# A two-layer attention and MLP kernel: the list scheduler gives way to written-out orders of each engine and a written-out list of PSUM banks

## The chip, the core and the metric

The kernel runs on one core of a Trainium2 chip. The core has five engines that run side by side, each through its own list of instructions in order: TensorE (PE in the profile, with PEld for its weight loads), VectorE (DVE), ScalarE (ACT), GpSimd (POOL) and SyncE (SP), which here issues every DMA. They wait for each other through semaphores. The metric is the device time of one execution in microseconds; lower is better. A measurement here is the median of several executions.

## What is computed

Input x is one sequence of 2048 rows of 576 bfloat16 numbers. Two layers are applied, each an attention block and an MLP block with residuals and the same weights in both layers:

```python
x = x + A(layernorm(x), wqkv, wo)
x = x + B(layernorm(x), w1, b1, w2, b2)     # and both once more

# A: 32 heads of 18, causal with a window of 256 keys
qkv = x @ wqkv
scores = q @ k^T * 18 ** -0.5, masked to 0 <= i - j < 256
o = softmax(scores) @ v, heads joined, @ wo
# B: layernorm again, then 576 -> 4608 -> 576
h = gelu(layernorm(x) @ w1 + b1)
out = h @ w2 + b2
```

## The kernel before, in words

**Tiles and chunks.** The 2048 rows are 16 tiles of 128; four tiles make a chunk, so there are eight chunks, 0 to 3 of the first layer and 4 to 7 of the second (`CH`). The residual x stays in SBUF in float32 (`x_res`), both layers run in one launch.

**What one chunk does.** The names are those of the stages in the code.

- `ln1`, `ln_stats`, `ln_rstd`, `ln_norm_T` (L690 to L749): layernorm. DVE takes mean and variance, POOL the reciprocal root, DVE writes the normalised tile `xn`, and a DMA turns it into `xnTa` (for attention) or `xnTm` (for the MLP). For the four tiles of the first chunk PE turns them instead (L742) and ACT copies them out of PSUM (L745).
- `qkv` (L838 to L885): q, k and v of a tile. In chunks 0 and 1 each is two halves of 288 columns with five matmuls (kinds f and c below, L804, L785, L788); from chunk 2 on each is two phases of row-halved matmuls (kind h, L844) where the second phase (`own=True`) waits for the first. DVE or ACT casts the halves into `qn` or `vA`, and a DMA turns q and k (L884); the k of the first chunk are turned on PE (L878) and copied by ACT (L882).
- `E`, `E0` with `scores` and `pv` (L900 to L1018): attention, for eight groups of heads in three parts. A `scores` task writes two pairs of PSUM banks (L913), ACT takes two exps of them (L922), POOL masks them (L943), and a `pv` task (L960) multiplies by v. DVE then transposes, divides and transposes again.
- `tail` (L1033): the product with wo, the residual add (L1023), and the second layernorm.
- `G_part` (L1055 to L1101), three times per chunk, `ga`, `gb`, `gc`: twelve blocks of w1 in kind h (L1080), each followed by a gelu on ACT (L1090). Two phases again, of 10 and 8 matmuls per task.
- `mm2` (L1103 to L1138), `ma`, `mb`, `mc`: the product with a third of w2, in two tasks of six blocks for each half of the columns, and the residual add on DVE.

The stages of neighbouring chunks are woven: while the attention of chunk k runs, the MLP of chunk k-1 and the projections of k+1 fill PE.

**Kinds of matmul task.** Every PE task has a `mode`: f (whole array), r (four row groups, `scores`), h (two row halves) or c (column groups: `pv`, `mm2`, `tail` and chunk 1's projections). A c task other than `pv` may also run as whole-array matmuls ("wide", L785) or as quads of four 32-column matmuls (L788), which the end of `schedule` chooses: runs of c tasks without a `pv`, and the parts of a run ahead of its first and behind its last `pv` when they sum to over 4 us, become wide.

**What sets the order.** `Plan.add` (L209) only collects tasks: what each reads and writes, an estimated cost and latency, a priority and the PSUM banks that it may have. `Plan.schedule` (L263 to L414) then simulates the engines: it takes again and again the task that can start first, with ties settled by `prio`, to which `PL.nudge` (L483 to L552) adds a number per stage, and `place` gives it the bank that is free earliest. Chains (`fifo`) hold the feeding matmuls and ACT's work in order of their listing; `starves` holds back tasks that would delay them before a planned 40 us; `turn` makes a change of kind dearer; `SWITCH` is its cost. Where PE would stand still in the plan for over 0.4 us before 140 us, `keep_warm` (L249) puts matmuls on zeros (`warm_fn`, L687). The tasks are then handed, sorted by their planned start, to the five lists, and `Sched.add` (L65) derives the semaphore waits from what they read and write. On the chip only the order within each list and the banks are left of the plan.

**The start.** SP issues the loads of x tile 0, x tile 1, the q weights (3 issues), the k weights (3), x tiles 2 and 3, the v weights (3), then x tiles 4 to 7. DVE clears `warm`, `ident`, and parts of wqkv and wo; PE then clears PSUM banks 7, 6, 5 and 4 with two matmuls each (`zero`, L675) and runs fillers.

Of the kernel before, what the change touches and what calls it, by code (L numbers as in the profile page):

```python
# [159 lines left out]
class Task:  # L160
    __slots__ = ("idx", "eng", "fn", "reads", "writes", "cost", "lat", "prio", "dma", "ring", "handles", "alloc", "move", "desc",
                 "npred", "succ", "ready", "end", "plain", "fifo", "hold", "stage", "mode", "own", "port", "wide")
# [24 lines left out]
class Plan:  # L187


    def __init__(self, S, nbanks):  # L190
        self.S = S
        self.tasks = []
        self.lw = {}
        self.rd = {}
        self.nbanks = nbanks
        self.warm_fn = None
        self.warm_from = 0.0
        self.warm_until = 0.0
        self.feed_until = 0.0
        self.turn = {}  # L200
        self.turn_from = 0.0
        self.ring = RING
        self.stage = ""
        self.part = ""
        self.chain = None
        self.nudge = {}
        self.fifo_last = {}

    def add(self, eng, fn, reads=(), writes=(), dma=None, ring=4, cost=0.1, lat=0.1, prio=0.0, alloc=(), fifo=None, plain=False, after=(), move=0.0, desc=0, hold=False, mode="f", own=False, port=None, wide=None):  # L209
        if eng == "dve" and fifo is None:  # L210
            fifo = self.chain
        stage = self.stage + self.part + ("+" if dma in ("w1", "w2", "xr") else "")
        prio += self.nudge.get(stage, 0.0)
        t = Task(idx=len(self.tasks), eng=eng, fn=fn, reads=tuple(reads), writes=tuple(writes), cost=cost, lat=lat, prio=prio,
                 dma=dma, ring=ring, alloc=tuple(alloc), handles=tuple({r for r in tuple(reads) + tuple(writes) if isinstance(r, Bank)}),
                 plain=plain, move=move, desc=desc, fifo=fifo, hold=hold, stage=stage, mode=mode, own=own,
# [16 lines left out]
        order = set()  # L233
        if fifo is not None:
            if fifo in self.fifo_last:
                order.add(self.fifo_last[fifo])
            self.fifo_last[fifo] = t
        order -= pred
        for p in pred:
            p.succ.append((t, True))  # L240
        for p in order:
            p.succ.append((t, False))
        t.npred = len(pred) + len(order)
# [5 lines left out]
    def keep_warm(self, a, b, bank_free, extra):  # L249

        if self.warm_fn is None or a < self.warm_from:
            a = max(a, self.warm_from)
        n = int((b - a - 0.1) * 0.8 / (0.165 if a < 7 else 0.115))
        banks = [x for x in (7, 6, 5, 4) if bank_free.get(x, 1e9) <= a]
        if n < 1 or not banks:
# [4 lines left out]
                 dma=None, ring=4, alloc=(), handles=(), plain=False, move=0.0, desc=0, fifo=None, hold=False, stage="", mode="f", own=False, port=False, wide=None)  # L260
        extra.append((a, t))

    def schedule(self):  # L263
        free = {e: BEGIN for e in ENGS}
        mode = "f"
        port = 0.0
        released = {e: [] for e in ENGS}
        for t in self.tasks:
            if t.npred == 0:
                released[t.eng].append(t)  # L270
        bank_free = {b: 0.0 for b in range(self.nbanks)}

        def place(t):

            got = []
            taken = set()
            when = 0.0
            for h in t.alloc:
                best = None
                for n, c in enumerate(h.choices):  # L280
                    bs = (c, c + 1) if h.pair else (c,)
                    if any(b in taken or b not in bank_free for b in bs):
                        continue
                    key = (max(bank_free[b] for b in bs), n)
                    if best is None or key < best[0]:
                        best = (key, c, bs)
                if best is None:
                    return None, None
                got.append(best[1])
                taken.update(best[2])  # L290
                when = max(when, best[0][0])
            return got, when

        feed = [t for t in self.tasks if t.fifo == "pa"]
        fed = 0
        backlog = 0.0

        def cost(t):
            return t.cost + (SWITCH if t.eng == "pe" and t.mode != mode else 0.0)

        def starves(t, st, got):

            if fed == len(feed) or feed[fed].npred:
                return False
            f = feed[fed]
            where, when = place(f)
            if where is None:
                return False
            at = max(free["pe"], f.ready, when)
            end = st + cost(t)  # L310
            late = end if at < end else at
            if t.alloc and set(got) & {b for w, h in zip(where, f.alloc) for b in ((w, w + 1) if h.pair else (w,))}:
                late = max(late, end + 0.65)
            return late > at and late + f.cost + f.lat > max(free["act"], st) + backlog

        order = []
        extra = []
        queued = {}
        served = {}
        turned = {}  # L320
        n = len(self.tasks)
        while len(order) < n:
            best = None
            cands = []
            for e in ENGS:
                for t in released[e]:
                    st = max(free[e], t.ready)
                    if t.port:
                        st = max(st, port)
                    got = ()  # L330
                    if t.alloc:
                        got, when = place(t)
                        if got is None:
                            continue
                        st = max(st, when)
                    key = (int((st + (self.turn.get(mode + t.mode, 0.0) if e == "pe" and st >= self.turn_from else 0.0)) * 1000 + 0.5), t.prio, t.idx)
                    if e == "pe":
                        cands.append((key, t, st, got))
                    if best is None or key < best[0]:
                        best = (key, t, st, got)  # L340
            assert best is not None, "stuck"
            _, t, st, got = best
            if t.eng == "pe" and t.fifo is None and st < self.feed_until and starves(t, st, got):
                for c in sorted(cands, key=lambda c: c[0]):
                    if c[2] < self.feed_until and (c[1].fifo is not None or not starves(*c[1:])):
                        _, t, st, got = c
                        break
            if t.eng == "pe":
                t.cost, mode = cost(t), t.mode
            if t.eng == "pe" and st < self.warm_until and st - free["pe"] > 0.4:  # L350
                self.keep_warm(free["pe"], st, bank_free, extra)
                free["pe"] = st
            released[t.eng].remove(t)
            for h, no in zip(t.alloc, got):
                h.no = no
                for b in h.banks():
                    del bank_free[b]
            free[t.eng] = st + t.cost
            if t.port:
                port = st + t.cost  # L360
            if t.fifo == "pa":
                fed += 1
                backlog += sum(x.cost for x, data in t.succ if data and x.eng == "act")
            elif t.fifo == "act" and t.handles:
                backlog -= t.cost
# [958 lines left out]
```

## Time and profile before

| | |
|---|---|
| median of 3 runs | 862.02 us (861.75 to 862.07) |
| span of the profiled execution, first to last instruction | 860.3 us |
| its own time beside the span | not given separately; the median of the runs stands 1.7 us above the span |
| PE busy | 849.0 us (99%), 11684 matmuls |
| ACT busy | 594.1 us (69%) |
| DVE, POOL busy | 393.9 us, 377.9 us |
| DMA moved | 119.78 MB, mean 139 GB/s |
| granted PE clock, mean over the span | 1.000 |

The profile describes one execution. A busy time is the union of the instructions of an engine; matmuls are pipelined, so a busy PE is not PE at its peak. "Idle before" is the time in which an engine had nothing running just ahead of an instruction, with the event that ended it. The chain of waits follows the work that ended last back to the start. The costliest groups are the MLP's first product and ACT's exps:

```profile
L1080 PE MATMUL ps<-xnTm,w_sb 64*128 64x512 bf16 x2592 | 289.2, 376 | 0.7 <-DVE x_res L1023 0.6
L922 ACT ACTIVATE pT<-ps 128x1024 bf16<-128x1024 f32 (+1 forms) x384 | 346.6, 973 | 59.3 <-PE ps L913 58.4
```

### The profile page before, as it was taken

To read this page: it belongs to the slowest core of one execution; us is meant where nothing else is said; L and a number is where in the kernel's file an instruction comes from. 1 tells how busy PE (TensorE), PEld (TensorE's weight loads), DVE (VectorE), ACT (ScalarE), POOL (GpSimd) and SP (SyncE) were. 2 spreads that over 40 slices of the span, in tenths; PEclk is the share of its full clock that TensorE was granted. 3 is DMA by queue.
4 is the path that set the end of the run, shared out by engine and by line. 5 is a ranking of instruction groups with operands and counts; after the bars stand their busy time and mean duration, and the time that the engine had idled before them with its cause. 6 is when DMAs were issued, how large, how long until landed. Compare 5 with 4: busy or idle time off the path is not lost.

```text
span 860.3 us, 27204 instructions
## 1 busy us (share of the span) xinstructions
PE 849.0 (99%) x11684; PEld 521.0 (61%) x11684; DVE 393.9 (46%) x934; ACT 594.1 (69%) x741; POOL 377.9 (44%) x560
## 2 busy tenths in 40 slices
PE   8999999999999999999999999999999999999998
PEld 6555556656556665565566665756556656656556
DVE  6778424655228543383254832654234434243012
ACT  3986887768667697477763977538777689772730
POOL 4777644465135662165330953426444276222100
PEclk9999999999999999999999999999999999999999
DMA  7896735371584734936347554484436854555320
GB/s 187 197 137 97 231 126 150 107 163 44 166 166 123 167 102 123 206 87 183 125 134 175 116 113 150 77 213 116 135 125 114 210 150 148 161 166 149 117 83 28
DMA packets 181863, 119.78 MB, mean 139 GB/s; under 512 B 107440, under 2 KB 181744, under 8 KB 181744
## 3 DMA queue, kind: packets, MB, share of 16 engines
q1 hardware_dynamic: 181744, 118.05, 54.1%
q8 instruction: 92, 1.51, 0.7%
q14 instruction: 27, 0.22, 0.1%
HBM read 90.10 MB, written 2.36 MB: 107 GB/s over the span
## 4 chain that ended last, share of the span: by engine, by line
PE 93%; ACT 3%; issue 1%; DVE 1%; SPq 1%; DMA 1%; POOL 0%; POOLq 0%
PE ps L1080 33%; PE ps L785 30%; PE ps L788 9%; PE ps L844 9%; PE ps L913 6%; PE ps L960 5%; ACT pT L922 2%; SPq L637 1%; DMA x_res<-in_A_x_dram 1%; PE ps L804 1%; ACT kT L882 0%; POOL pT L943 0%; DVE oq L971 0%; DVE x_res L1023 0%; ACT hT L1090 0%
## 5 line engine op out<-in xcount | busy, mean ns | idle before, releaser
L943 POOL TENSOR_SCALAR_AFFINE_SELECT pT<-pT 128x512 bf16<-128x512 bf16 (+1 forms) x368 | 283.8, 792 | 238.9 <-ACT pT L922 234.4
L922 ACT ACTIVATE pT<-ps 128x1024 bf16<-128x1024 f32 (+1 forms) x384 | 346.6, 973 | 59.3 <-PE ps L913 58.4
L1080 PE MATMUL ps<-xnTm,w_sb 64*128 64x512 bf16 x2592 | 289.2, 376 | 0.7 <-DVE x_res L1023 0.6
L1090 ACT ACTIVATE hT<-ps,b1col 128x512 bf16<-128x512 f32 x276 | 167.4, 687 | 167.1 <-PE ps L1080 166.6
L1080 PEld LDWEIGHTS ps<-xnTm,w_sb 64*128 64x128 bf16 x2592 | 128.7, 94 | 144.5 <-issue 6.0
L785 PE MATMUL ps<-w_sb,hT 128*128 128x288 bf16 x1482 | 198.4, 287 | 0.0
L1023 DVE TENSOR_TENSOR x_res<-ps,x_res 128x288 f32<-128x288 f32 x224 | 100.0, 450 | 191.6 <-PE ps L785 155.7
L785 PEld LDWEIGHTS ps<-w_sb,hT 128*128 128x128 bf16 x1482 | 137.4, 98 | 51.2 <-issue 15.8
L844 PE MATMUL ps<-wqkv,xnTa 64*128 64x288 bf16 x1296 | 90.3, 283 | 0.9 <-DVE x_res L1023 0.3
L865 DVE CAST qn<-ps 128x288 bf16<-128x288 f32 x120 | 49.0, 450 | 89.4 <-PE ps L844 82.8
L788 PE MATMUL ps<-w_sb,hT 128*32 128x288 bf16 x2520 | 87.9, 287 | 0.5 <-ACT hT L1090 0.5
L971 DVE STREAM_TRANSPOSE oq<-ps 128x512 f32<-128x512 f32 x64 | 45.8, 715 | 84.9 <-PE ps L960 84.1
L844 PEld LDWEIGHTS ps<-wqkv,xnTa 64*128 64x128 bf16 x1296 | 61.7, 94 | 28.3 <-issue 2.5
L788 PEld LDWEIGHTS ps<-w_sb,hT 128*32 128x32 bf16 x2520 | 64.8, 97 | 14.0 <-issue 3.9
L913 PE MATMUL ps<-qT,kT 32*128 32x384 bf16 (+2 forms) x1216 | 64.1, 276 | 1.4 <-ACT pT L922 1.3
L713 POOL TENSOR_SCALAR vtmp<-mv_all 128x1 f32<-128x1 f32 (+1 forms) x43 | 8.9, 207 | 121.9 <-DVE mv_all L704 119.5
L852 DVE CAST vA<-ps 128x288 bf16<-128x288 f32 x64 | 26.8, 449 | 63.3 <-PE ps L844 59.8
L700 DVE BATCH_NORM_STATS2 st_all<-x_res 128x6 f32<-128x288 f32 (+1 forms) x128 | 53.2, 442 | 3.7 <-DMA x_res<-in_A_x_dram 2.8
L1096 POOL TENSOR_TENSOR x_res<-x_res,b2bc 128x576 f32<-128x576 f32 x32 | 40.4, 1281 | 28.6 <-ACT hT L1090 28.6
L960 PE MATMUL ps<-pT,vA 128*20 128x384 bf16 (+2 forms) x1408 | 50.4, 276 | 0.0
L913 PEld LDWEIGHTS ps<-qT,kT 32*128 32x128 bf16 x1216 | 19.4, 92 | 41.8 <-issue 27.3
L785 PE MATMUL ps<-wo_sb,attT 128*128 128x288 bf16 x320 | 41.6, 287 | 0.0
(56 smaller groups left out, 469.5 us busy)
## 6 DMA issues: line engine op xcount, KB each, us to landing
w_sb<-in_B_w_dram SPq DMA_DIRECT2D x46, 864.0 KB, 5.8
w_sb<-in_B_w_dram SPq DMA_DIRECT2D x48, 768.0 KB, 4.7
w_sb<-in_B_w_dram SPq DMA_DIRECT2D x96, 48.0 KB, 4.4
wqkv<-in_A_wqkv_dram SPq DMA_DIRECT2D x3, 576.0 KB, 5.6
x_res<-in_A_x_dram SPq DMA_DIRECT2D x3, 576.0 KB, 4.5
out_dram<-x_res SPq DMA_DIRECT2D x12, 144.0 KB, 1.9
wqkv<-in_B_w_dram SPq DMA_DIRECT2D x2, 864.0 KB, 4.9
wo_sb<-in_A_wo_dram SPq DMA_DIRECT2D x4, 144.0 KB, 5.1
```

Source lines behind the costliest of these rows:

```text
L700: add("dve", lambda e, i=i, s=s: e.bn_stats(st_all[:, t, i, :], s[:, t, i * HB:(i + 1) * HB]), reads=res, writes=[f"st{t}_{i}"], cost=0.37 ...
L785: return e.matmul(bank(b)[:, 0:HB], lhs, rhs, start=start, stop=stop, skip_group_check=True)
L788: ins = e.matmul(bank(b)[32 * j:32 * j + 32, 0:HB], lhs[:, 32 * j:32 * j + 32], rhs, start=start, stop=stop, tile_position=(0, 32 * j), sk ...
L844: ins = e.matmul(bank(bs[o])[:, 0:HB], xnTa[r:r + 64, c, i * 128:(i + 1) * 128], wqkv[r:r + 64, c, col:col + HB], start=(c == 4), stop=(ph ...
L865: add("dve", lambda e, b=bs[o], dst=dst: e.tensor_copy(dst, heads_of(bank(b))), reads=[bs[o]], writes=[f"qn{sl}h{o}"], cost=0.375, lat=0.1 ...
L913: ins = e.matmul(two(bs[j // 2])[:, j % 2, col:col + nq * 128], k_of(T0 + so)[0][32 * j:32 * j + 32, g, :], qs[32 * j:32 * j + 32, g, qo * ...
L922: add("act", lambda e, h2=h2: e.activation(pT[:, sl, 2 * h2:2 * h2 + 2, lo:hi], two(bs[h2])[:, :, lo:hi], ACT.Exp, scale=SCALE), reads=[bs ...
L943: add("pool", lambda e, ap=ap, pat=pat, sgn=sgn, kind=kind: e.affine_select(ap, ap, pattern=pat, compare_op=(ALU.is_ge if kind == "d" else ...
L960: ins = e.matmul(bank(bo)[32 * j:32 * j + VW, qo * 128:(qo + nq) * 128], vA[:, (T0 + so) % VS, 8 * j + g, :], pT[:, sl, j, col:col + nq * ...
L1023: add("dve", lambda e: e.tensor_tensor(x_res[:, t, sl], bank(b)[:, 0:HB], x_old[:, t, sl], ALU.add), reads=[b] + ([f"xin{t}"] if first els ...
L1080: ins = e.matmul(bank(bks[i])[:, 0:n], w1_sb[r:r + 64, sls[i], col:col + 128], xnTm[r:r + 64, k % 2, c, 0:n], start=(c == 4), stop=(ph == ...
L1090: add("act", lambda e, ff=ff, hd=hd, bk=bk: e.activation(hd[:, 0:n], bank(bk)[:, 0:n], ACT.Gelu_apprx_tanh, bias=b1col[:, ff:ff + 1]), rea ...
```

## The change

The tasks stay the same, except that PE now clears all eight PSUM banks at the start, not four: four more tasks, so that a task numbered N from 30 on has the number N + 4. `schedule` no longer chooses. It reads five written-out lists of task numbers, `ORDER`, and a string of one bank per allocation, `BANKS`, and walks through them to get planned times, which still place the fillers and choose wide or quad. `fifo`, `starves`, `turn` and the nudges are gone. A few estimates change (cost of a matmul, of a clearing, latency of w2 and of a transposing DMA, `SWITCH` from 0.095 to 0.103), as does the count of fillers in a planned gap. The lists are close to the order before: of PE's 1201 old tasks 951 keep their relative order, of ACT's 741 it is 600, of DVE's 934 it is 503, of POOL's 556 it is 316, of SP's 353 it is 159; a PE task moves by 4.2 places in the mean.

The diff, cut to what the prediction speaks of (`...` marks what is left out):

```diff
     def keep_warm(self, a, b, bank_free, extra):
-        if self.warm_fn is None or a < self.warm_from:
-            a = max(a, self.warm_from)
-        n = int((b - a - 0.1) * 0.8 / (0.165 if a < 7 else 0.115))
+        a = max(a, self.warm_from)
+        if a >= b:
+            return
+        n = int((b - a - 0.1) * (0.95 / 0.2135 if a < 6 else 0.8 / 0.115))
...
     def schedule(self):
+
+        tasks = self.tasks
+        seq = {e: deque(spread(ORDER[e])) for e in ENGS}
+        assert sorted(i for q in seq.values() for i in q) == list(range(len(tasks))) and len(BANKS) == len(self.given)
+        for h, b in zip(self.given, BANKS):
+            h.no = int(b)
...
             for e in ENGS:
-                for t in released[e]:
...
+                if not seq[e]:
+                    continue
+                t = tasks[seq[e][0]]
+                need = [b for h in t.alloc for b in h.banks()]
+                if t.npred or any(b not in bank_free for b in need):
+                    continue
+                st = max([free[e], t.ready, port if t.port else 0.0] + [bank_free[b] for b in need])
+                if best is None or st < best[0]:
+                    best = (st, t)
...
-SWITCH = 0.095
+SWITCH = 0.103
...
+def spread(s):
+    for x in s.split():
+        a, _, b = x.partition("-")
+        yield from range(int(a), int(b or a) + 1)
+
+ORDER = {
+    "pe":
+        "27 31 29 33 26 28 32 30 43 44 77 83 82 57 58 78 86 93 67 68 92 89 107 108 113 72 73 112 103 88 104 116 98 97 164 122 "
+        "169 123 127 174 128 134 101 131 133 118 179 119 184 346 345 192 351 350 188 197 206 356 355 211 383 201 230 235 384 "
...
+        "476 438 784 785 789 485 790 794 795 481 490 798 803 799 804 495 808 505 809 500 510 523-526 534 533 536 535 546-549 "
...
+        "654 648 656 647 655 649 657 665-668 677 730 614 731 733 734 682 748 749 687 751 752 692 736 737 701 739 740 706 742 "
...
+    "act":
+        "34 42 45 56 85 59 80 66 95 69 71 87 110 115 74 117 100 165 166 170 125 171 175 130 176 102 132 180 181 185 186 194 "
...
+    "dve":
+        "13 22 25 35-37 23 41 46 40 47 55 79 50-52 84 60 61 65 62 148 144 70 94 145 24 109 141 139 147 142 146 105 114 138 91 "
...
+    "sp":
+        "0 2 1 4 3 5-8 76 10 11 9 81 96 111 137 126 157 163 154 160 349 220 225 219 327 335 223 340 406 354 227 228 403 226 "
...
+        "519 521 543 644 802 555 643 774 788 664 663 662 807 755 673 877 879 674 793 754 823 675 835 847 859 1000 889 878 896 "
...
+        "2617 2645 2612 2640 2529 2606 2607 2675 2631 2659 2687 2748 2654 2751 2699 2540 2711 2731 2754 2757 2740 2729 2844 "
+        "2730 2741 2868 2822 2742 2845 2869 2878 2880 2867 2965 2966 2879 2843 2984 2996 2986 2985 3102 2997 3069 3074 2829 "
...
+}
...
-    PL.nudge = {"": -92.05, "b": -19.76, "ea0.0": 28.56, "ea0.1": -4.45, "ea0.2": 114.56, "ea0.p0": -14.45, "ea0.p2": 33.51,
...
+    ZERO = (7, 6, 5, 4, 3, 2, 1, 0)
...
-        return max(n / 2400.0, 0.026) + (0.003 if n > 64 else 0.0)
+        return n / 2400.0 + 0.0023
...
-    for i in OUT:
+    for i in ZERO:
         b = Bank((i,))
-        add("pe", lambda e, b=b: zero(e, b), reads=["warm"], writes=[b], cost=0.25, lat=0.2, prio=-7, alloc=[b])
+        add("pe", lambda e, b=b: zero(e, b), reads=["warm"], writes=[b], cost=0.43, lat=0.2, prio=-7, alloc=[b])
```

Who is who at the places that the prediction names, in the new numbers: 164 is the first scores task; 43, 44, 57, 58, 67, 68, 72, 73 turn the first four xn tiles; 77, 78 are the q halves of tile 0, 82, 83 its k halves, 88, 89 its v halves, 86 and 116 turn the k of tiles 0 and 2, 101 and 131 those of tiles 1 and 3; 97 and 98 are k halves of tile 1, 134 a v half of tile 3; 100 is ACT's cast of half of tile 1's k into `qn`. 798 and 799 are the two phases of chunk 2's q of tile 3, 803 and 804 those of its k, 809 the second phase of its v; 505 and 510 are scores of chunk 1, 500 a pv of it. 730 and 731 are the two parts of the first `mb0.0` column half, 614 a pv of chunk 1; 646 is the first task of `gb0`. 1000 and 2844 load the first block of w2 (864 KB) for `ma1` and `ma5`, behind the first parts of `mc0` and `mc4` that still read its place; 878 and 2730 load 48 KB of w1 that `ga1.1` and `ga5.1` use.

210 lines of the change are left out of this document (60 added, 150 removed), and 212 rows, old and new, of tables (ORDER, add).

## The prediction, made before the changed kernel was run

> **What bounds the kernel now.** I read the page first, then the busy time by stretches, then the start in order of time, then the chain of waits.
>
> ```profile
> span 860.3 us, 27204 instructions
> PE 849.0 (99%) x11684; PEld 521.0 (61%) x11684; DVE 393.9 (46%) x934; ACT 594.1 (69%) x741; POOL 377.9 (44%) x560
> PE 93%; ACT 3%; issue 1%; DVE 1%; SPq 1%; DMA 1%; POOL 0%; POOLq 0%
> ```
>
> PE is busy for 849.0 of 860.3 us and holds 93% of the chain. A new order gains only what PE idles, what it spends between kinds of matmul, and filler that real work can replace. The stretches show where it idles (columns: stretch, length, then busy time and count of PE, PEld, DVE, ACT, POOL):
>
> ```profile
> 0.00:6.70 6.70, 5.66 (x27) 3.94 (x28) 3.75 (x12) 1.53 (x2) 4.37 (x17) 1.00 0.71 193
> 6.70:21.30 14.60, 12.95 (x120) 9.32 (x118) 10.60 (x33) 6.26 (x13) 4.40 (x10) 1.00 0.76 185
> 21.30:51.00 29.70, 27.28 (x417) 16.16 (x416) 22.19 (x57) 28.88 (x43) 22.81 (x38) 1.00 0.90 181
> 51.00:86.40 35.40, 33.92 (x543) 20.37 (x545) 28.94 (x75) 25.36 (x30) 23.95 (x39) 1.00 0.73 115
> 86.40:140.00 53.60, 52.83 (x718) 30.44 (x718) 19.52 (x43) 46.84 (x58) 28.80 (x36) 1.00 0.52 162
> 140.00:700.00 560.00, 559.49 (x8259) 345.10 (x8258) 265.16 (x620) 396.68 (x485) 254.43 (x372) 1.00 0.56 138
> 700.00:857.20 157.20, 156.85 (x1616) 95.64 (x1612) 43.32 (x97) 88.53 (x115) 39.13 (x54) 1.00 0.41 130
> ```
>
> From 6.7 to 140 us PE idles 1.65 + 2.42 + 1.48 + 0.77 = 6.3 us; from 140 to its end at 857.2 only 0.51 + 0.35 = 0.9. The first 6.7 us are clearing and filler, the last 3.1 the closing add and the store. From 21.3 to 51 another engine is the limit: ACT is busy 28.88 of 29.70. So the sum below is mostly one over the first 140 us.
>
> **The change part by part.** Task numbers are the new list's; from 30 on they are the old ones plus four.
>
> *Head, to the first scores (task 164).* In order of time:
>
> ```profile
> 1.15 0.98 DVE L669 MEMSET wqkv<- 64x432 uint32 x2
> 2.72 4.15 PE L687 MATMUL ps<-warm 128*128 128x256 bf16 x19
> 5.19 0.43 DVE L725 TENSOR_SCALAR xn<-x_res,mv_all,rstd 128x576 bf16<-128x576 bf16 x1 [0.73 <-POOL rstd L715]
> 5.88 1.67 SPq L637 DMA_DIRECT2D wqkv<-in_A_wqkv_dram  x3
> 6.71 0.44 PE L742 MATMUL ps<-ident,xn 128*128 128x128 bf16 x5
> 6.99 0.49 PE L687 MATMUL ps<-warm 128*128 128x256 bf16 x3
> 9.49 1.11 PEld L804 LDWEIGHTS ps<-wqkv,xnTa 128*128 128x128 bf16 x10 [0.43 <-DMA wqkv<-in_A_wqkv_dram]
> 13.57 1.18 DVE L700 BATCH_NORM_STATS2 st_all<-x_res 128x6 f32<-128x288 bf16 x3 [0.71 <-DMA x_res<-in_A_x_dram]
> 15.50 0.48 PEld L804 LDWEIGHTS ps<-wqkv,xnTa 128*128 128x128 bf16 x5 [1.09 <-DVE qn L865]
> 15.76 4.32 PE L804 MATMUL ps<-wqkv,xnTa 128*128 128x288 bf16 x33
> 21.35 0.34 PE L913 MATMUL ps<-qT,kT 32*128 32x384 bf16 x4
> 22.76 0.42 ACT L862 CAST qn<-ps 128x288 bf16<-128x288 f32 x1
> ```
>
> xn0 is ready at 5.62, but PE transposes it at 6.71, behind 19 fillers of 4.15 / 19 = 0.218. In the new list `warm` is DVE's third memset, behind `ident` and one of two wqkv memsets of 0.49: clearing starts some 0.6 later than before, and its sixteen matmuls take 16 x 0.218 = 3.5, to about 5.2; less filler fits behind them. So the four added banks (8 x 0.218 = 1.7) cost nothing as long as xn0 comes at 5.62; without that cover, 1.7. The transposes start near 5.7, a gain of 1.0 that does not last: the k weights are SP's sixth issue in both lists and land near 9.45, and the new list puts both k halves (83, 82) ahead of the second q half (78).
>
> From 9.49 the new list has, up to the scores, 15 projection halves of 5 matmuls at (4.32 - 0.29) / 32 = 0.126, so 9.45, and 15 + 16 transposing matmuls at about 0.055 (five in 0.44 with the last one's 0.22), so 1.7. Sum 11.2: the scores start at 20.7, not 21.35, with one more half (98) done ahead of them. That needs the 1.09 wait at 15.50 gone. DVE sat at 13.57 waiting for x tiles 4 to 7, with xn3 and a q cast queued behind. That load moves on SP from thirteenth to tenth, past the three v issues (1.67 in all); the v weights' first use moves back, to task 89. And xn1 no longer queues behind the statistics of tile 2. Gain 0.65; bounds 0 (another wait replaces it) and 1.3 (the extra half counts in full).
>
> *First chunk's attention, to 51 us.* ACT's stretch: what counts is when its exps start and what else it must do among them. A qn cast (100; 0.42 by the row) moves ahead of the first exp. ACT's own idle is 29.70 - 28.88 = 0.82; of it I take 0.3, since projection 134 now stands ahead of the transposes 101 and 131, which follow ACT's casts. Bounds beyond the head: 0 and 0.42 + 0.82 = 1.2. Head and attention: 0.65 + 0.42 + 0.3 = **-1.4** (0 to -2.5).
>
> *51 to 86.4.*
>
> ```profile
> 67.64 0.54 PE ps L687 x4
> 82.74 0.83 DVE qn L865 x2
> 83.71 0.42 PE ps L913 x8
> 84.15 1.03 ACT pT L922
> 85.23 0.40 PE ps L913 x8
> ```
>
> Filler holds 0.54 and idle is 1.48. The list puts pv 500 between scores 505 and 510, which stood an exp apart with PE waiting; but 500 follows at once on 809, whose cast (0.42, half of the second row) must first free a bank, so most of that is lost again. Projections now alternate (798 803 799 804) where 798 and 799 were neighbours, the second half waiting for the first. I take **-0.9**; bounds 0 and -2.0 (both numbers whole).
>
> *86.4 to 140.*
>
> ```profile
> 115.53 0.47 DVE x_res L1023
> 128.85 0.71 ACT hT L1090
> 129.60 2.39 PE ps L788 x72
> 131.99 0.65 PE ps L960 x24
> ```
>
> The second part of `mb0.0` waits for gelus until 129.60. The new list has 730 614 731: the 0.65 pv steps into that wait. And `gb0.0` (646) takes bank 1 in place of 7, which DVE had only just read (first row); I give that 0.25. **-0.9**; bounds 0 and -1.1 (the pv and the whole DVE add).
>
> *After 140.* The order of kinds is almost the old one. **-0.3**; bounds 0 and -0.9, all idle.
>
> *Changes of kind on PE.*
>
> ```profile
> 106.11 0.33 PE ps L913 x8
> 106.44 1.58 PE ps L785 x12
> 750.89 1.58 PE ps L788 x48
> 769.75 16.77 PE ps L785 x136
> 786.52 23.42 PE ps L1080 x216
> ```
>
> Undisturbed, a 288-column matmul takes 16.77 / 136 = 0.123, and 512 columns 2 x 23.42 / 216 = 0.217 (two run side by side). A score task of 512 columns with twelve matmuls would be 0.217 + 1.48 = 1.70; they take 1.91. Two changes cost 0.21, one about 0.11. Counted along the lists by the tasks' kinds f, r, c, h, there are 411 now and 409 after: **-0.2**. How they spread over pairs of kinds I bound by 0 and three times that, -0.6. That ten fewer c tasks run as quads is worth nothing: 48 narrow and 12 wide matmuls both take 1.58.
>
> *New waits.* SP's list is the most changed, and SP issues in order. Two small w1 loads (2730 for chunk 5, 878 for chunk 1) now stand right behind a w2 load (2844, 1000) that waits for the first part of an mm2 task.
>
> ```profile
> DMA to landing us min/median/max: 3.8/4.7/8.1
> 598.32 1.12 SPq L637 DMA_DIRECT2D w_sb<-in_B_w_dram  x2
> 599.27 7.08 PE L1080 MATMUL ps<-xnTm,w_sb 64*128 64x512 bf16 x64
> ```
>
> The w2 load of chunk 4 went out at 598.32; the w1 load would go 0.56 later, at 598.9. Its user is the sixth half from 599.27, behind 10 + 10 + 8 + 8 + 10 matmuls at 0.108: 604.2. That leaves 5.3: 0.6 to spare at the median landing, 2.8 too late at the slowest. Behind 864 KB it is rather late: **+0.4** for the two; bounds 0 and 5.2.
>
> Sum: -1.4 - 0.9 - 0.9 - 0.3 - 0.2 + 0.4 = **-3.3**, so 860.3 - 3.3 = 857.0 for the span. The median 862.0 stands 1.7 above the profiled span; I keep that distance: **858.7**.
>
> **The rivals.**
>
> *More is gained (855.7).* All idle and filler that the lists touch goes: -2.5 - 2.0 - 1.1 - 0.9 - 0.2 + 0.4 = -6.3. For it: a busy PE hides waits. The 136 matmuls above start 0.123 apart, but the page gives such a matmul 287 ns, so a wait up to 0.16 leaves no idle in the stretches. The Trainium skill, "Perfetto Trace Analysis", Identifying the Most-Contended Engine, says the same: matmul busy time is no good measure of distance from the roof, since matmuls are pipelined; by that rule the late stretches' 99.9% need not be full, which speaks for this rival. Against: the late lists keep their order of kinds. Chance 0.20.
>
> *The head pays back (861.2).* The clock. Fillers go from 0.218 to about 0.11 (three in 0.49, the last one's tail in it) only between 6.87 and 6.99, after PE had worked without a break since it began to clear. The new list starts later and has a hole between the first q half and the k halves at 9.49. If the ten k matmuls and the transposes behind them ran at half rate, they would take 1.26 + 0.72 = 2.0 longer, ahead of the first exp; with a wait like that of 15.50 in part uncured, 2.5. 858.7 + 2.5 = 861.2. Against: the planner puts fillers into holes that it foresees. Chance 0.17. The Trainium skill, "TensorE: Matmul & The Clock Gate", Part 1, gives the full clock after a busy window of about 3.4 us and the half clock after an idle one; the trace shows the first and, before its end, no loss. By that window one miss would cost an estimated 1.7.
>
> *Slower (863.9).* The two w1 loads land as the slowest row does, at 8.1: 2.8 late, and about 2.4 for 878: 858.7 + 5.2 = 863.9. It decides at a landing of 5.3 after issue. For it: 864 KB just ahead in the queue, and a list in which any late load would do the same; against: the median of 4.7. Chance 0.13.
>
> **How the numbers follow.** Forecast 858.7, its own range with the small terms between their bounds 857 to 860.3: 0.50. More: 0.20. The head pays back: 0.17. Slower: 0.13. The range 854.8 to 861.9 takes in the second and third and leaves out the slower one and a little more. A measurement tells 0.2% (1.7 us) from no change: faster is below 860.3, slower above 863.7. Faster 0.50 + 0.20 = 0.70, same 0.17, slower 0.13.
>
> **What would show it.** Transposes of xn0 near 5.7; k halves still near 9.5; first scores near 20.7 without a DVE wait of 1 us ahead of them; the first chunk's exps over near 49.6; a pv where PE waited at 128; the stretches from 140 on as long as before; PE idle ahead of L1080 at chunks 1 and 5 that ends with a w1 DMA would show the new wait. Wrong if the idle removed before 140 us comes back as waits on ACT or DVE, if fillers still take 0.2 past 7 us, or if the late stretches shrink: then waits inside the busy time were missed.

## The result, and the profile after

The changed kernel takes 860.28 us, the median of 13 runs (859.55 to 860.88); the kernel before, in 13 runs beside it, 862.07 (861.55 to 863.02). The ratio is 0.9978 with a 95% interval of 0.9970 to 0.9986: 1.8 us faster, where 3.3 were forecast; 860.28 lies on the edge of the forecast's own range, 857 to 860.3. The profiled execution spans 858.5 us, 1.8 below the median.

First the page, then the busy time by the same stretches as before (length, then busy time and count of PE, PEld, DVE, ACT, POOL; granted PE clock, DMA share, GB/s):

```profile
span 858.5 us, 26755 instructions
PE 846.7 (99%) x11500; PEld 521.2 (61%) x11500; DVE 384.8 (45%) x934; ACT 596.1 (69%) x741; POOL 371.3 (43%) x560
```

```profile
6.70:21.30 14.60, 12.74 (x121) 9.76 (x120) 11.03 (x35) 7.45 (x16) 4.12 (x9) 1.00 0.82 215
21.30:51.00 29.70, 28.34 (x424) 16.93 (x422) 23.88 (x61) 28.38 (x41) 22.94 (x38) 1.00 0.59 95
51.00:86.40 35.40, 33.41 (x539) 19.80 (x539) 29.60 (x75) 25.24 (x30) 22.89 (x39) 1.00 0.73 141
86.40:140.00 53.60, 53.30 (x763) 31.85 (x762) 15.04 (x39) 47.37 (x59) 30.50 (x38) 1.00 0.54 163
```

The idle time of PE falls from 2.42 to 1.36 between 21.3 and 51, and from 0.77 to 0.30 between 86.4 and 140. Between 51 and 86.4 it rises, from 1.48 to 1.99: the filler of 0.54 is gone, but nothing took its place.

Stretches of fixed times mix the work of two orders. The starts of the same task in both traces say it better. The lead is the start before less the start after:

| task | before | after | lead | gained since the row above | forecast |
|---|---|---|---|---|---|
| first scores, 164 | 21.35 | 20.43 | 0.92 | 0.92 | 0.65 |
| scores 291, near 51 us | 52.59 | 51.34 | 1.25 | 0.33 | 0.72 |
| first gate task `ga0.0`, 523 | 86.33 | 84.94 | 1.39 | 0.14 | 0.9 |
| `gc0.0`, 861 | 144.89 | 142.96 | 1.93 | 0.54 | 0.9 |
| `ga5.0`, 2847 | 599.27 | 596.90 | 2.37 | 0.44 | |
| `ga5.1`, 2858 | 604.24 | 602.19 | 2.05 | -0.32 | -0.4 (two loads) |
| pv 3255 | 711.28 | 709.62 | 1.66 | -0.39 | |
| end of PE's last task | 857.19 | 855.60 | 1.59 | -0.07 | |

The tail of add and store is 0.15 shorter too (2.92 against 3.07 us), which makes 1.74 between the two profiled spans. So the gain is made ahead of 143 us, as forecast; the stretch from 51 to 86.4 brought a sixth of its term, and behind 143 the lead first grows by 0.44 and then falls by 0.78.

Each trace is one execution, so a row that rests on one landing of a DMA can differ in the next. The row of 0.54 does not: from `ga0.0` to `gc0.0` five further traces of the new order (e5, e7, e9, e10, e11) take 58.02 too, and e1, in the old order, 58.56 like the kernel before. The split between the first two rows does: in e1 the first scores start at 21.61, behind five fillers, and scores 291 at 52.52, so that against e1 the scores lead by 1.18 and the attention adds nothing (30.91 in both). Their sum stands: scores 291 start between 52.52 and 52.72 in the three traces of the old order and between 50.97 and 51.76 in the nine that have the new order up to there and its fillers.

The head, in order of time:

```profile
1.63 3.37 PE L700 MATMUL ps<-warm 128*128 128x256 bf16 x16 [1.63 <-DVE warm L695]
4.84 0.49 PE L709 MATMUL ps<-warm 128*128 128x256 bf16 x3
5.68 0.51 PE L761 MATMUL ps<-ident,xn 128*128 128x128 bf16 x5 [0.35 <-DVE xn L744]
6.02 0.71 PE L709 MATMUL ps<-warm 128*128 128x256 bf16 x5
7.01 0.77 PE L823 MATMUL ps<-wqkv,xnTa 128*128 128x288 bf16 x5 [0.28 <-ACT xnTa L764]
9.37 1.39 PE L823 MATMUL ps<-wqkv,xnTa 128*128 128x288 bf16 x10 [1.58 <-DMA wqkv<-in_A_wqkv_dram]
20.43 0.34 PE L932 MATMUL ps<-qT,kT 32*128 32x384 bf16 x4
21.69 0.34 PE L932 MATMUL ps<-qT,kT 32*128 32x384 bf16 x4 [0.20 <-ACT pT L941]
```

Clearing starts 0.6 later, the transposes come at 5.68, the k halves at 9.37; up to the scores no wait of 1 us is left. The second score task already waits for ACT: from here the exps set the pace.

The two spots of the old chain that the new order was to mend, and the gate task at 115 (chain of waits: start, length, what):

```profile
82.04 0.40 PE ps L932 x8
82.43 0.61 PE ps L863 x8
83.05 0.03 issue
83.07 0.47 DVE vA L871
83.54 0.14 issue
83.68 0.83 PE ps L978 x24
84.51 0.33 PE ps L932 x8
84.84 0.10 issue
84.94 2.10 PE ps L1098 x17
```

```profile
126.89 0.85 PE ps L807 x24
127.75 0.72 PE ps L978 x24
128.47 2.21 PE ps L807 x72
```

```profile
114.73 1.47 PE L1098 MATMUL ps<-xnTm,w_sb 64*128 64x512 bf16 x12 [0.30 <-ACT pT L941]
```

At 83 pv 500 stands between the scores, but waits 0.65 for DVE to read bank 6 behind projection 809. At 128 the pv (L978) fills the old wait of 0.47. At 114.73 `gb0.0`, no longer in the bank that DVE had to read, waits 0.30 for ACT, which reads its other bank, 0.

### The profile page after: what moved, and what is told of

Its sections match the earlier page's. It is cut to its first block, busy times and chain, and to the rows that moved or that the text cites. A ratio compares the mean times of both kernels' runs of the same rounds, so it can differ in the third digit from the quotient of the medians.

```text
span 858.5 us, 26755 instructions
## 1 busy us (share of the span) xinstructions
PE 846.7 (99%) x11500; PEld 521.2 (61%) x11500; DVE 384.8 (45%) x934; ACT 596.1 (69%) x741; POOL 371.3 (43%) x560
## 4 chain that ended last, share of the span: by engine, by line
PE 93%; ACT 2%; issue 1%; DMA 1%; DVE 1%; POOL 1%; SPq 0%
PE ps L1098 33%; PE ps L804 30%; PE ps L863 10%; PE ps L807 8%; PE ps L932 6%; PE ps L978 5%; ACT pT L941 2%; PE ps L823 1%; POOL pT L961 1%; DMA wqkv<-in_A_wqkv_dram 1%; DMA xnTm<-xn 0%; SPq L659 0%; ACT hT L1108 0%; DVE oq L989 0%; DVE xn L744 0%
## 5 line engine op out<-in xcount | busy, mean ns | idle before, releaser
L961 POOL TENSOR_SCALAR_AFFINE_SELECT pT<-pT 128x512 bf16<-128x512 bf16 (+1 forms) x368 | 280.3, 785 | 238.7 <-ACT pT L941 233.9
L1108 ACT ACTIVATE hT<-ps,b1col 128x512 bf16<-128x512 f32 x276 | 169.5, 687 | 162.2 <-PE ps L1098 161.8
L804 PE MATMUL ps<-w_sb,hT 128*128 128x288 bf16 x1542 | 205.8, 287 | 0.0
L804 PEld LDWEIGHTS ps<-w_sb,hT 128*128 128x128 bf16 x1542 | 143.5, 98 | 52.2 <-issue 15.2
L863 PE MATMUL ps<-wqkv,xnTa 64*128 64x288 bf16 x1296 | 92.2, 283 | 0.9 <-DVE x_res L1041 0.3
L884 DVE CAST qn<-ps 128x288 bf16<-128x288 f32 x120 | 50.8, 448 | 83.6 <-PE ps L863 78.3
L807 PE MATMUL ps<-w_sb,hT 128*32 128x288 bf16 x2280 | 79.2, 286 | 0.0
L807 PEld LDWEIGHTS ps<-w_sb,hT 128*32 128x32 bf16 x2280 | 58.7, 97 | 11.9 <-issue 3.3
L978 PE MATMUL ps<-pT,vA 128*20 128x384 bf16 (+2 forms) x1408 | 50.4, 276 | 0.8 <-DVE vA L871 0.6
```

The lines of the kernel that those rows point to most:

```text
L804: return e.matmul(bank(b)[:, 0:HB], lhs, rhs, start=start, stop=stop, skip_group_check=True)
L807: ins = e.matmul(bank(b)[32 * j:32 * j + 32, 0:HB], lhs[:, 32 * j:32 * j + 32], rhs, start=start, stop=stop, tile_position=(0, 32 * j), sk ...
L863: ins = e.matmul(bank(bs[o])[:, 0:HB], xnTa[r:r + 64, c, i * 128:(i + 1) * 128], wqkv[r:r + 64, c, col:col + HB], start=(c == 4), stop=(ph ...
L884: add("dve", lambda e, b=bs[o], dst=dst: e.tensor_copy(dst, heads_of(bank(b))), reads=[bs[o]], writes=[f"qn{sl}h{o}"], cost=0.375, lat=0.1 ...
L961: add("pool", lambda e, ap=ap, pat=pat, sgn=sgn, kind=kind: e.affine_select(ap, ap, pattern=pat, compare_op=(ALU.is_ge if kind == "d" else ...
L978: ins = e.matmul(bank(bo)[32 * j:32 * j + VW, qo * 128:(qo + nq) * 128], vA[:, (T0 + so) % VS, 8 * j + g, :], pT[:, sl, j, col:col + nq * ...
```

## The experiments

All times are against the kernel before, run beside each (862.2 to 862.4); the changed kernel stands at -1.8. The edits are shown against the changed kernel. "Splice" means that each of the five lists is taken from one order up to a task and from the other behind it, the banks with them.

**e1: the old order in the changed code.**

```diff
-        "27 31 29 33 26 28 32 30 43 44 77 83 82 57 58 78 86 93 67 68 92 89
+        "27 31 29 33 26 28 32 30 43 44 77 78 82 83 86 57 58 88
```

> The changed code (eight banks cleared, the new rule for fillers) with the five task lists and the PSUM banks that the list scheduler had chosen. Theory (the order makes the difference; the clearing lies behind the load and normalization of x tile 0, ready at 5.62): 862.1, within 0.4 of the kernel before, the transposes of xn0 near 5.7, the scores still near 21.3 because the k weights land near 9.5 in any case. Rival A (the clearing and the fillers make the difference): 860.3. Rival B (eight more clearing matmuls without cover): 862.1 + 1.7 = 863.8.

862.44 against 862.41, ratio 1.0002 (0.9993 to 1.0011). The transposes come at 5.70 and the scores at 21.61. So the four more banks cost nothing, and the whole difference is the order, with its banks. (Of the 4.2 places that a PE task moves in the mean, all but 0.9 are the shift by the four added clearing tasks.)

**e2, e3, e4: splices.** The seam of e2 in PE's and SP's list:

```diff
 pe  ... 164 122 169
-    123 127 174 128 134 101 131
+    123 127 174 128 101 131 133
 sp  ... 111 137
-    126 157 163 154 160 349 220
+    154 157 126 227 228 229 163
```

> The new lists up to the second score task (PE to task 169, ACT to 166, DVE to 121, POOL to 168, SP's first 17 issues), the old ones behind. Theory (a lead gained ahead of the first score is carried through the rest one to one): 862.1 - 1.25 = 860.8, the lead at 50 us 0.9 to 1.3. Rival (ACT, busy 28.9 of 29.7 us there, swallows the lead in the first chunk's attention): 862.0, lead under 0.3 at 50 us.

> The new lists up to the last pv task of chunk 1's first attention pass (PE to task 711, about 142 us), the old ones behind. Theory (the whole net gain stands by 142 us: 1.93 in the traces): 862.1 - 1.9 = 860.2, or lower by what the new late lists lose: no wait for a w1 load at chunk 5, no wait of 0.5 ahead of chunk 6. Rival (the gain is spread over all chunks, 142 of 860 us hold a sixth): 861.8.

> The opposite splice: the old lists up to the same tasks, the new ones behind. Theory: 862.1 + 0.0 to + 0.3 (the traces give the late lists +0.45 by 597 us, -0.33 at the late w1 load, -0.57 at the late transposed xn, +0.2 at the end), so 862.0 to 862.5. Rival (spread gain): 860.6.

All three missed, at the seams. e2: 866.97, ratio 1.006 (1.0047 to 1.0072). Its lead is 1.33 at the seam; then SP stands 6.2 us at 154, which the old list has first and which waits for PE, and the transposed q that score 179 reads (126) goes out behind it. SP's wait from 18 to 36 us and PE's from 24 to 40 (total, times, longest):

```profile
SPq L132 <- PE ps L882: 6.2, 1, 6.2
```

```profile
PE ps L917 <- DMA qT<-qn: 3.9, 1, 3.9
```

The wait takes the lead from 1.62 to -2.37; 2.84 more goes while the granted clock stands at 0.50, from 29.62 to 36.45. From the task that the kernel before starts at 33.24 on the lead is -5.21, and at PE's last task it is -5.21 still: the rest of the kernel carries a shift of any size through, neither gaining nor losing. That much of the theory it shows; the rival's number was as far off. e3: 863.56 (1.0001 to 1.0019). The lead of 1.47 at 140 us is -0.15 at `gc0.0`, since the last pv of the new list and the first gate task of the old one both use bank 3 (0.9 of waiting for DVE), and 1.7 more goes at 786 to a transposing DMA that landed late (in the profiled execution, 864.17; e3's runs spread from 862.09 to 864.18). e4: 866.29 (1.0036 to 1.0061), with the same conflict in bank 7 (1.9) and 2.4 more by 180 us. Neither says anything on the lists behind the seam.

**e9: the splice at a clean seam**, in the middle of attention-free gate work where both orders write banks 0 to 3.

```diff
 pe  ... 880-883
-    812 813 824 825 906 836 837 848 911 849 976 916
+    812 813 824 825 906 836 837 848 849 911 973 974
```

> The splice of the third run with a cleaner seam: the new lists up to the end of chunk 0's third gate stage (PE to task 883, ACT to 886, DVE to 715, POOL to 893, SP to its 77th issue), where both orders write the same four banks next, the old ones behind. Theory (the whole net gain stands by 155 us, and the new lists behind it win nothing): the lead at 155 us 1.7 to 2.0, the same lead at 700 us; 1.9 below the kernel before (1.5 to 2.3 with the spread of the DMA landings), level with the changed kernel. Rival (the late lists hold part of the gain): 0.9 or less below.

860.69, ratio 0.9982 (0.9973 to 0.9991): 1.5 below, within the bounds given and level with the changed kernel. The lead is 2.16 at 157 us, 1.94 at 166 and 1.93 at PE's last task; the profiled execution is the fastest of its runs (859.96). The gain stands whole by 155 us; what the new late lists win they lose again.

**e5: the second q half in the hole ahead of the k halves.**

```diff
-        ... 43 44 77 83 82 57 58 78 86
+        ... 43 44 77 78 83 82 57 58 86
-        "34 42 45 56 85 59 80 66
+        "34 42 45 56 80 85 59 66
```

> The changed kernel with the second q half of x tile 0 (task 78) ahead of the k halves 83 and 82, and its cast (80) two places earlier on ACT. Theory (from the k halves at 9.37 to the first scores at 20.43 PE is busy without a hole, so a half of 0.62 that fills part of the hole of 1.58 ahead of them moves all that follows): k halves still at 9.4, scores at 19.8, the lead 0.62 larger to the end; 2.4 below the kernel before, where the changed one is 1.8 below. Rival (another engine is due there: DVE's or ACT's casts, the x tiles): a new wait takes the 0.62, 1.8 below.

860.69, ratio 0.9982 (0.9973 to 0.9991); scores at 20.48. The rival holds. PE in order of time:

```profile
7.27 2.64 PE L823 MATMUL ps<-wqkv,xnTa 128*128 128x288 bf16 x20 [0.20 <-issue]
9.75 0.44 PE L761 MATMUL ps<-ident,xn 128*128 128x128 bf16 x5
10.86 0.62 PE L897 MATMUL ps<-ident,qn 128*128 128x128 bf16 x8 [0.67 <-DVE qn L884]
...
13.52 1.77 PE L823 MATMUL ps<-wqkv,xnTa 128*128 128x288 bf16 x13 [0.41 <-DMA wqkv<-in_A_wqkv_dram]
```

The half had covered the 0.67 for the cast of k, and then PE stands 0.41 for the last v load (task 9), moved on SP from tenth to thirteenth. The test is not a clean one: here the last k load landed at 8.39, in the changed kernel's trace at 9.23, so that half of the hole was gone already. But the v load ends the head either way. In the changed kernel it lands at 13.32 and the first v half (task 89) starts at 13.43, in e7 13.25 and 13.29, in e8 13.02 and 13.06, in e9 13.21 and 13.26, in e11 13.73 and 13.78; the first scores follow the landing by 7.00 to 7.11 in these five. Idle time of PE ahead of task 89 shows only in e5 (0.41) and e11 (0.56). In the other four with the new head, e2, e3, e6 and e12, task 89 starts 0.15 to 0.29 behind the landing and the scores 7.13 to 7.35: something else came last there.

**e6: pv 500 in bank 5.**

```diff
-    BANKS: task 500 -> 6
+    BANKS: task 500 -> 5
```

> The changed kernel with pv task 500 in bank 5 in place of 6, which projections 808 and 809 still hold. Theory (the wait of 0.65 ahead of 500 at 83.03 is for DVE to read bank 6): 500 starts at 83.1; the score task behind it then waits for ACT to free bank 0 at about 84.0, so 0.4 of the 0.65 is left: 2.2 below the kernel before. Upper bound: all 0.65, 2.45 below. Rival (ACT, without idle time from 80.96 to 84.73, sets the end of this stretch): the wait moves to the score task whole, 1.8 below.

862.77, ratio 1.0009 (1.0000 to 1.0018): slower than the changed kernel, against both. Bank 5 was not free: score task 505 has banks 0 and 4, and each stands for a pair, so ACT reads 5 later than DVE reads 6. PE in order of time, then stretches:

```profile
82.79 0.66 PE L863 MATMUL ps<-wqkv,xnTa 64*128 64x288 bf16 x8
85.20 1.16 PE L978 MATMUL ps<-pT,vA 128*20 128x384 bf16 x24 [1.75 <-ACT pT L941]
```

```profile
82.00:84.00 2.00, 1.21 (x20) 0.42 (x16) 0.61 (x3) 2.00 (x3) 1.64 (x2) 1.00 0.65 128
84.00:85.00 1.00, 0.00 (x0) 0.00 (x0) 0.78 (x3) 1.00 (x2) 0.00 (x0) 1.00 0.37 72
85.00:85.60 0.60, 0.40 (x12) 0.27 (x16) 0.00 (x0) 0.15 (x1) 0.38 (x1) 0.97 0.00 0
85.60:88.80 3.20, 3.20 (x34) 1.14 (x28) 1.43 (x3) 1.84 (x2) 0.25 (x1) 0.50 0.78 225
```

The wait is 1.75 where it was 0.65. And then the granted clock falls to 0.50 for the 3.2 us behind it: from pv 500 to the second gate task PE takes 3.75 in place of 2.34, so the wait cost 1.4 more than itself. Nine of e6's eleven runs have a mean clock of 0.998, as this one; the two at 1.000 take 861.53 and 862.57.

**e7: two late waits.**

```diff
 sp
-    ... 2740 2729 2844 2730
+    ... 2740 2729 2730 2844
 pool
-    ... 3164 3165 3233 3167
+    ... 3164 3165 3167 3233
```

> The changed kernel with two orders mended that only its late waits concern: the w1 load 2730 (chunk 5) ahead of the w2 load 2844 on SP, and the copy 3167 (chunk 6's fourth normalized tile) ahead of a mask on POOL. Theory (each wait is the load or copy that stands behind another one in its list): the 0.33 at 601.9 and most of the 0.53 at 696.7 go, 1.8 + 0.33 + 0.5 = 2.6 below the kernel before. Rival (the landing, not the issue, sets both: a transposing DMA takes 2.6 to 6.9 us here): only the first or none goes, 1.8 to 2.1 below.

859.92, ratio 0.9974 (0.9964 to 0.9983): 2.4 below. In the changed kernel the small w1 load, issued at 596.35 right behind 864 KB, landed 5.75 later, and PE broke off ahead of its sixth half; in e7 it went out at 586.7 and PE ran on. The changed kernel's PE, its load from issue to landing (KB, us), then e7's PE:

```profile
596.90 5.14 PE L1098 MATMUL ps<-xnTm,w_sb 64*128 64x512 bf16 x46
602.19 4.06 PE L1098 MATMUL ps<-xnTm,w_sb 64*128 64x512 bf16 x36 [0.15 <-issue]
```

```profile
w_sb<-in_B_w_dram SPq DMA_DIRECT2D x1, 48.0 KB, 5.8
```

```profile
598.70 5.56 PE L1098 MATMUL ps<-xnTm,w_sb 64*128 64x512 bf16 x50
```

PE's time from `ga5.0` to the sixth half shrinks from 5.29 to 4.97, by 0.32, as the theory has it, and that stays. But the wait is one of some executions. Six more traces have this load right behind the 864 KB:

| | e10 | e4 | e5 | e8 | e12 | e6 | changed |
|---|---|---|---|---|---|---|---|
| issue to landing | 4.70 | 4.77 | 4.91 | 5.38 | 5.50 | 5.61 | 5.75 |
| time beyond 4.97 up to the sixth half | 0 | 0 | 0.01 | 0 | 0.05 | 0.15 | 0.32 |

So a landing within 5.4 costs nothing, and e7's 0.4 over the changed kernel, which the intervals do not tell from nothing, cannot be put down to this load alone. In e7 it goes out 1.7 behind 768 KB and takes 6.25 to land; it is harmless because it goes out 10 us earlier. The wait at 697 did not go. Its row (PE's waits from 690 to 700 us) reads the same in both, here e7's:

```profile
PE ps L1098 <- DMA xnTm<-xn: 0.5, 1, 0.5
```

The transposing DMA went out 0.8 earlier and took 4.4 to land in place of 3.8; before the change it took 2.6. The new SP list issues a w load 1.3 us behind it in both; the old one at 2.8. For this wait the rival holds. All traces with the new list there (e4, e5, e6, e8, e10, e11 and e12 beside these two) have PE idle for 0.40 to 1.04, and the DMA lands 3.7 to 4.4 behind its issue; why it lands late is open, since elsewhere in the changed kernel an xn DMA with a w load 1.30 behind it (583.00) landed in 2.57.

**e8 and e12: pv 614 back behind 734.**

```diff
-        730 614 731 733 734 682
+        730 731 733 734 614 682
 e12 only:
-    BANKS: 730 -> 0, 733 -> 7, 614 -> 1
+    BANKS: 730 -> 7, 733 -> 6, 614 -> 7
```

> The changed kernel with pv task 614 back behind the mm2 tasks 730 to 734, as in the old order; the planner then puts two fillers into the wait at 128. Theory (the pv fills the wait for the gelus): the lead falls from 1.38 + 0.55 to 1.38 at 140 us and stays there, 1.25 below the kernel before. Rival (the 0.55 comes from another part of the stretch): 1.8 below.

> The changed kernel with pv task 614 behind 734 as in the old order, tasks 730, 733 and 614 in the banks of the old order (7, 6, 7), and DVE's read of 614 behind that of 734, so that no score task waits for the pv's bank. Theory (the pv fills the wait at 128 and nothing else): the lead falls by 0.55 to 0.6 at 128 and stays so, 1.2 below the kernel before, where the run with 614 in bank 1 lost 1.46 more to the score task behind it. Rival (a pv task anywhere else costs a wait of its own): 0.3 above to 0.3 below.

e8: 863.10 (1.0002 to 1.002). It loses 0.58 against the changed kernel at the wait for the gelus, and 1.46 more because score 682 needs the pair 0 and 1, which DVE now frees late: 614 writes bank 1, and the add that reads 730 in bank 0 stands behind DVE's work on 614. e12 takes that conflict away: 861.09, ratio 0.9988 (0.9979 to 0.9996), 1.1 below. From `ga0.0` to `gc0.0` it takes 0.55 longer than the changed kernel. The step is worth what its wait was, and the order and the banks belong together. e12's PE:

```profile
127.23 0.92 PE L807 MATMUL ps<-w_sb,hT 128*32 128x288 bf16 x24 [0.16 <-ACT hT L1108]
128.39 2.39 PE L807 MATMUL ps<-w_sb,hT 128*32 128x288 bf16 x72 [0.24 <-ACT hT L1108]
```

**e10: no filler.**

```diff
-WARM_UNTIL = 140.0
+WARM_UNTIL = 0.0
```

> The changed kernel without any filler matmul (the planned time up to which fillers are put is 0), so that PE's holes between 5.0 and 9.4 and two of 0.2 to 0.3 in the first chunk stay empty. Theory of the clock (the grant near 6.9 comes from unbroken work): the clearing of 3.4 alone is too short, the k halves and what follows run at half rate until about 12.8, the first scores come about 1.7 later: level with the kernel before, 0.0 to 0.3 above it. Rival (the sixteen clearing matmuls have the clock granted by themselves, and the holes are too short to lose it; what limits the head is the landing of the weights): 1.8 below, as the changed kernel.

862.58, ratio 1.0007 (0.9998 to 1.0015): the whole gain is gone. Stretches of e10, then of the changed kernel:

```profile
5.00:9.00 4.00, 1.58 (x13) 0.87 (x12) 2.26 (x6) 1.18 (x3) 0.89 (x3) 1.00 1.05 289
9.00:9.60 0.60, 0.60 (x5) 0.46 (x6) 0.00 (x0) 0.00 (x0) 0.00 (x0) 0.82 1.08 385
9.60:12.80 3.20, 3.20 (x19) 2.23 (x18) 2.66 (x9) 1.09 (x2) 0.74 (x2) 0.50 0.83 289
```

```profile
5.00:9.00 4.00, 2.15 (x19) 1.15 (x16) 2.25 (x6) 1.18 (x3) 0.83 (x3) 1.00 1.04 306
9.60:12.80 3.20, 3.20 (x38) 2.75 (x36) 2.92 (x10) 1.72 (x5) 0.93 (x3) 1.00 0.82 281
```

PE is busy in both rows of 3.2 us, but at clock 0.50 it gets 19 matmuls done, not 38. From the k halves to the scores it takes 12.67 in place of 11.06. So the k halves ran at half rate until 12.80, as the theory of the clock has it, but not for its reason: the clock stood at 1.00 from 5.98 on, so the clearing matmuls had it granted by themselves, as the rival says, and at 9.39 the holes lost it again.

The scores come 1.20 later, `ga0.0` 1.96, PE's end 2.18. The step from 1.20 to 1.96 is no clock: PE idles 0.89 ahead of `ga0.0`, 0.10 in the changed kernel, until 0.46 behind the landing of the transposing DMA 448, which SP issued at 83.87, 1.96 later than in the changed kernel. And the trace speaks for some of the executions: of e10's twelve runs five have a mean clock below 1.000 (0.996 to 0.998), this one among them; the seven at 1.000 are no faster (861.4 to 865.2), and what they lost is not shown. What the two fillers of the first chunk's small holes have of it was not told apart.

**e11: the w1 load, and POOL's copies ahead of its masks.** SP's list has the edit of e7.

```diff
 pool
-    ... 444 489 445 423 459 480 447
+    ... 444 445 423 489 459 447 480
```

> The changed kernel with the w1 load 2730 ahead of the w2 load 2844, and on POOL the copies 423 and 447 (normalized tiles of chunk 0) ahead of the masks 489 and 480. Theory (ga0.0, the first gate task, starts 0.46 behind the landing of the transposing DMA 448, in every run of the new order so far near 84.5, so that a larger lead is given back there): 448 lands 0.6 to 0.8 earlier, ga0.0 then follows the score task 510 without a wait: 0.1 to 0.45 more lead from 85 us on, and 0.34 more from 602: 2.2 to 2.6 below the kernel before. Rival (ACT's exps set the end of that stretch): the start of ga0.0 unchanged near 84.95, only the 0.34: 2.1 below.

860.34, ratio 0.9981 (0.9972 to 0.9989). `ga0.0` starts 1.00 behind the landing of 448, where it is 0.46 in the changed kernel, e3, e7, e8, e10 and e12: it is free of that DMA. But little was to be had. From the first scores to `ga0.0` it takes 64.45, e5, e9 and e12, whose copies were not moved, 64.42 to 64.47; the changed kernel takes 64.51, e3 64.68, e7 64.69, e8 64.89. What tells these apart is SP: it spent 1.5 to 1.8 us on the transposing DMA ahead of 448 (460) in e3, e7 and e8, 1.3 in the changed kernel and e12, 1.2 in e5, e9 and e11. Where 448 is not late, `ga0.0` follows ACT's exp 507 (it ends at 85.04 in e11, `ga0.0` starts at 85.19), so the rival holds for this part. The sixth half of `ga5` runs without a wait; the wait at 697 is 0.88.

## Why the forecast was right in sign and too large

**Head and first chunk, -1.4: right (-1.25).** Every point came in this execution: transposes at 5.68 for 5.7, k halves at 9.37 for 9.5, scores at 20.43 for 20.7, no wait of 1 us on DVE. The wrong share was inside: the head gave 0.92, and 1.18 against e1, the attention behind it 0.33, and nothing against e1, where 0.72 were forecast; ACT sets its pace from the second score task on. What replaced DVE's wait as the next limit, the v load behind the x tiles, was seen as moved and not as a limit; e5 and e11 show it.

**51 to 86.4, -0.9: the step that failed (-0.14).** It took filler and idle time of PE as something that a better order can fill. The filler at 67.64 covered a wait for data: the first wo task (425) keeps its distance to the last pv of the first chunk (318) in both traces, 4.25 and 4.27, and only moves with the head's lead. The pv between the scores was forecast to lose most of the gain again to a cast of 0.42; it lost 0.65, and with that more than there was to gain. Up to score 505 the lead had grown from 1.25 to 1.67; from 505 to `ga0.0` it takes 2.62 before and 2.90 after, so the step that was to bring the gain cost 0.28. Bank 6, for all that, was the better choice of the two tried (e6), and behind it stand ACT's exps and then, 0.1 later, the transposing DMA 448.

**86.4 to 140, -0.9: right in mechanism, one half too large (-0.54).** The pv in the wait at 128 was priced at 0.65; the trace gives 0.55 and e12 the same. The bank of `gb0.0`, 0.25, is worth nothing: the idle time ahead of it is 0.30 in both, DVE on bank 7 having hidden ACT on bank 0.

**New waits, +0.4: right in mechanism, the size partly luck (+0.32).** The load for chunk 5 landed 5.75 after its issue, beyond the 5.3 from which it was to decide, the one for chunk 1 landed 0.7 ahead of its use. e7 takes the wait away, and the table there bears out the 5.3; but in six more traces the same load cost 0 to 0.15.

**After 140, -0.3, and the kinds, -0.2: not told apart.** Up to chunk 5 the lead grows by 0.44, about their sum. What was missed is the wait for a transposed xn at 697, 0.53 here and 0.40 to 1.04 in eight more traces.

**The rivals.** "The head pays back" did not come, but e10 shows that it stood where it was put: 2.0 to 2.5 was its price, and an unfilled head cost 1.2 at the scores in e10's trace, less than forecast. The holes, not the later start of the clearing, were the danger. "Slower" asked for both w1 loads to be late by over 2 us; one was, by 0.3. "More is gained" fell with the stretch from 51 to 86.4. The best version measured is e7, 859.92 (2.4 below), too close to the changed kernel to call it better.

## What to carry to other kernels

A filler or a gap of the busiest engine is a gain only where nothing else is due: follow the task behind it to its input and ask whether that input moves too. Under a fixed order a lead is carried one to one, by 820 us of other work here, until a DMA that comes late takes it, so compare two traces by the start of the same task and not by stretches. Do it in several executions: the wait for the late w1 load stands in one trace and not in the next. Lists and banks fit only each other: three of four splices here and one changed bank failed by waits of their own.

## What the runs showed of the hardware

- The clock falls after less idle time than expected. A hole of 1.75, in a stretch from 82.0 to 85.6 in which PE was busy for 1.6 of 3.6, was followed by 3.2 us at clock 0.50 (e6). The Trainium skill, "TensorE: Matmul & The Clock Gate", Why this matters for your kernels, advises no idle gaps over about 3 us; these runs ask for less. The Trainium skill gives a window of about 3.4 us in Part 1 of the same page, and the length of the slow stretches agrees.
- As far as these traces tell, PE's busy share between two steps of the clock decides, not the longest hole: e10's longest was 1.05 and lost the clock, the changed kernel's 1.58 did not. The granted clock of these traces changes at steps of 3.41 us (5.98, 9.39 and 12.80 in e10; 85.56 and 88.98 in e6; 29.62 and, two steps on, 36.45 in e2). PE busy in a step, and the clock behind it; in e11 and the changed kernel the steps are counted on from the first grant, 5.96 and 4.64:

| | e2, 26.21 to 29.62 | e6, 82.15 to 85.56 | e10, 5.98 to 9.39 | e11, 5.96 to 9.37 | changed, 8.06 to 11.47 |
|---|---|---|---|---|---|
| busy of 3.41 us | 0.53 | 1.42 | 1.53 | 1.99 | 2.10 |
| clock behind it | 0.50 | 0.50 | 0.50 | 1.00 | 1.00 |

- Where the steps fall differs from execution to execution (first grant between 4.64 and 7.06 in the traces that show one), so the fillers make the loss of the clock rare and not impossible. From 5.98 to 9.39 PE is busy for 1.55 in the changed kernel too, as much as in e10; its steps fell elsewhere. In e7 and e11 one run of ten each has a mean clock of 0.998 and takes 861.76 and 861.95, 1.8 and 1.6 above the median; where in the run it fell is not shown.
- The same loads, issued at the same times to 0.04, land up to 1.4 apart: the last k load between 8.13 and 9.54 in executions of the new head with its fillers, the last v load between 13.02 and 13.73. The first scores start between 20.08 and 20.87 and move with the v load: the earliest k load (e6) has the latest scores.
- An xn transposing DMA lands in 2.5 to 9.2 us in these traces. The slow ones that stand out went out 0.6 behind a load of 768 or 864 KB: 8.30 and 7.08 (before, 284.82 and 387.85), 6.96 and 6.86 (changed kernel, 181.22 and 517.86). A load 1.3 behind it need not hurt: 2.57 and 2.60 (changed kernel, 583.00 and 285.70).
